# A linear-attention and expert kernel on one core: float64 weights joined in one VectorE pass, 1/E by backward scans, a new order table

## The chip, the core and the metric

The kernel runs on one core of one Trainium2 chip. The metric is the device time of one execution in microseconds (us), from the first to the last instruction of the program. TensorE does the matrix products (PE in the profile, PEld its weight loads), VectorE (DVE), ScalarE (ACT) and GpSimd (POOL) the elementwise work, and SyncE (SP) issues almost all transfers. Each engine runs its own instructions strictly in the order in which the program holds them, and waits on semaphores for the others.

## The reference

```python
def _attn_ref(r, k, v, w, u):                 # B, H, S, D = 4, 8, 768, 48
    state = np.zeros((B, H, D, D))
    for t in range(S):
        cur = np.einsum('bhd,bhe->bhde', u[None] * kt, vt)
        y[:, :, t] = np.einsum('bhd,bhde->bhe', rt, state + cur)
        state = wt[:, :, :, None] * state + np.einsum('bhd,bhe->bhde', kt, vt)

def _moe_ref(x, w_in, w_out):                 # x: 3072 x 384, w_in: 384 x 2048, w_out: 2048 x 384
    h = np.maximum(x @ w_in, 0.0)
    return (h * h @ w_out).astype(np.float32)
```

The attention output, laid out as 3072 tokens of 384 values, is the input x of the second part. r, k, v, w and u are float32. w_in and w_out arrive as float64, since a float32 array is multiplied by a float64 number when they are drawn; the kernel has to make float32 numbers out of their eight bytes, and then splits each of them into a leading and a remaining part of the matmul's reduced type (float32r), so that three matmuls with the two parts give nearly the float32 product.

## The kernel before

The sequence of 768 steps is cut into six chunks (c = 0 to 5) of 128. A **unit** (c, b) is one chunk of one of the four batches, 24 units in all. The attention of a unit works on four pairs of heads at once (NP = 4), with 112 partitions that hold two heads of 48 channels. It takes E, the running product of w along the chunk; r times E (shifted by one) and k divided by E are then multiplied on TensorE to give the scores inside the chunk, with a mask, a diagonal term from u, and the state that comes from the chunk before.

The steps carry names, which are also the keys of the order table: `load` (w, k and r into the tile st), `turn` (chunk 0 alone: TensorE transposes into the banks ob0 to ob3, hp0, hp1 and a0), `z` and `pt` (the other chunks: VectorE transposes blocks of 32, and 16 SP transfers spread them into pt), `scan` (E: four scans of 128 on VectorE, line 411), `ln` (ScalarE: Ln of E and Exp of its negative, lines 418 and 419, which is 1/E), `rt` (r times E, 422), `kn` (a Newton step on 1/E in two VectorE passes, 428 and 429, and k times the result, 431), `rk` (two GpSimd passes, 438 and 440, over r, k and u), `beta` (their sum, 441), `diag` (ScalarE, 448), `far` (a guard that tells whether the inputs allow this method, 450 and 451; otherwise a slow branch at the end runs, which these inputs never take), `mt` (score matmuls, 459), `mask` (463), `ktp`, `kt`, `dS`, `S` (the new state), `mix` (the output matmuls) and `x`, `x3` (output split into its two parts).

The second part walks over 16 slices f of 128 of the 2048 hidden columns for each chunk, with two slices to a weight group g (g = 0 to 7). In the profile, `hp` is the first product (line 573, nine matmuls), then ScalarE takes the maximum with zero (578), VectorE squares (579), ScalarE and VectorE split the result into g's two parts (581, 582), and `ob` is the second product (588, three matmuls for each batch, added up in the banks ob0 to ob3 over all f). In chunk 0 the first six slices (groups 0 to 2) are done in two halves, first for batches 0 and 1, then for batches 2 and 3 (`HALF`); a matmul of hp then has 256 columns in place of 512.

The weights are loaded once, in chunk 0, and stay in SBUF. A group has two halves, ri (for w_in, becomes wi) and ro (for w_out, becomes wo), each 128 partitions of 768 float64 numbers. A half goes through `split_w`:

```python
P.add("act", 0.8, rank, widen, r=parts, w=[q])       # high word times 2**-112
P.add("dve", 0.48, rank, shift, w=[q], port=True)    # three bits to the left
P.add("dve", 0.88, rank, sign, r=parts, w=[q], port=True)
P.add("dve", 0.88, rank, low, r=parts, w=[q], port=True)
```

These are lines 318, 322, 326 and 331. Then ScalarE casts the result to the leading part (338) and GpSimd subtracts it from the number itself, which leaves the remaining part (339). A matmul needs both parts.

What sets the order: every step is added to a `Plan` with its engine, a cost, a rank and the data that it reads and writes. `Plan.order` then plays the steps through with these costs, lets an engine take the ready step that can start first (of those the one with the smaller rank), and emits all instructions in the order that comes out. The numbers in `AT`, `AT0`, `U0`, `C1`, `WL`, `OFF`, `W0` and `LAG` are the ranks. The order on each engine is thus fixed when the program is built; on the chip nothing overtakes.

## Time and profile before

| what | value |
|---|---|
| time, median of 3 runs | 559.23 us (558.83 to 562.87) |
| span of the profiled execution | 559.93 us |
| busy: PE / DVE / ACT / POOL | 530.8 / 359.1 / 288.0 / 101.3 us |
| mean granted TensorE clock | 0.989 |
| transfers | 50.86 MB, mean 91 GB/s |

The page gives the busy time of each engine over the whole span. Since the work of chunk 0 differs from that of the later chunks, the busy times by stretch of the span say more than the sums. Matmuls overlap in the profile, so that the time one of them costs is the distance between two starts in the timeline, and not the duration in its row. A float32 matmul (not float32r) stands in the trace as two records. The groups of instructions are listed by line, with the mean duration of one.

### The profile page before, as it was taken

Reading aid. Unit: us, or ns where it says so; the run is one execution under the profiler, and the core shown is the slowest. Engines: PE = TensorE matmul, PEld = TensorE weight load, DVE = VectorE, ACT = ScalarE, POOL = GpSimd, SP = SyncE. Lnnn points to the kernel's source line nnn. Section 1 sums busy time; section 2 is a strip of 40 time slices with the busy share of each in tenths; the row PEclk is TensorE's granted clock in tenths of the full one; section 3 lists DMA queues with packets and bytes.
Section 4 is the critical chain, followed back from the end, with each engine's and each line's share of the span. In section 5 each row is a group of like instructions: output and inputs, shape, how many; then the busy total and the mean of one; then the engine's idle time right before and its main releaser. Section 6 shows DMA issues by size and latency. Waiting matters only on the chain. (4 is left out here: it accounts for less than half of the span.)

```text
span 559.9 us, 10076 instructions
## 1 busy us (share of the span) xinstructions
PE 530.8 (95%) x3800; PEld 466.7 (83%) x3800; DVE 359.1 (64%) x643; ACT 288.0 (51%) x677; POOL 101.3 (18%) x115
## 2 busy tenths in 40 slices
PE   4768898999999999999999999999999999999995
PEld 3557787889998999988888888888888888998994
DVE  5789879898759596776866767567475233332330
ACT  2786776668554747555554554553563222332322
POOL 4253552352203003030401102102000000000000
PEclk9998898999999999999999999999999999999999
DMA  9999699237472645637470470460440000010001
GB/s 156 210 240 217 122 255 218 39 64 137 99 141 51 111 109 91 123 78 135 80 132 2 78 168 24 84 129 2 78 106 3 12 1 1 14 58 2 0 1 60
DMA packets 206326, 50.86 MB, mean 91 GB/s; under 512 B 196032, under 2 KB 201152, under 8 KB 206272
## 3 DMA queue, kind: packets, MB, share of 16 engines
q1 hardware_dynamic: 205552, 49.17, 43.9%
q10 hardware_dynamic: 720, 0.98, 0.5%
q8 instruction: 32, 0.52, 0.4%
q14 instruction: 22, 0.18, 0.1%
HBM read 31.65 MB, written 4.72 MB: 65 GB/s over the span
## 5 line engine op out<-in xcount | busy, mean ns | idle before, releaser
L573 PE MATMUL hp<-x,wi 128*128 128x512 f32 (+1 forms) x1062 | 225.6, 358 | 4.7 <-DVE g L582 4.7
L588 PE MATMUL ob<-wo,g 128*128 128x384 f32 x1152 | 224.7, 341 | 4.4 <-ACT g L581 4.4
L588 PEld LDWEIGHTS ob<-wo,g 128*128 128x128 f32 x1152 | 200.5, 189 | 12.2 <-ACT g L581 4.9
L573 PEld LDWEIGHTS hp<-x,wi 128*128 128x128 f32 x1062 | 175.5, 190 | 31.9 <-DVE g L582 5.8
L579 DVE SCALAR_TENSOR_TENSOR hp<-hp,t 128x512 f32<-128x512 f32 (+1 forms) x118 | 70.2, 596 | 110.5 <-ACT t L578 110.0
L578 ACT ACTIVATE t<-hp 128x512 f32<-128x512 f32 (+1 forms) x118 | 60.9, 516 | 136.8 <-PE hp L573 111.2
L582 DVE TENSOR_TENSOR g<-hp,g 128x512 fp32r<-128x512 f32 (+1 forms) x118 | 69.1, 586 | 37.7 <-ACT g L581 35.9
L581 ACT CAST g<-hp 128x512 fp32r<-128x512 f32 (+1 forms) x118 | 59.2, 504 | 54.6 <-DVE hp L579 54.4
L448 ACT ACTIVATE m<-ident,beta 128x128 f32<-128x128 f32 x192 | 60.5, 395 | 7.0 <-DVE beta L441 7.0
L438 POOL TENSOR_TENSOR st<-st 128x384 f32<-128x384 f32 x24 | 25.1, 1047 | 64.7 <-DVE st L367 63.5
L463 DVE COPY_PREDICATED m<-caus,a 128x512 f32<-128x512 uint8 x48 | 33.0, 731 | 5.5 <-PE a L459 5.5
L459 PEld LDWEIGHTS a<-pt 48*128 48x128 f32 x384 | 25.8, 199 | 11.4 <-issue 7.1
L459 PE MATMUL a<-pt 48*128 48x128 f32 x384 | 30.8, 298 | 4.4 <-DVE pt L431 4.4
L526 DVE SCALAR_TENSOR_TENSOR x<-a,x 112x128 fp32r<-112x128 f32 (+2 forms) x44 | 17.9, 432 | 20.5 <-ACT x L525 19.9
L493 PE MATMUL a<-m,v 128*48 128x128 f32 (+1 forms) x384 | 28.5, 291 | 2.3 <-DVE m L463 1.8
L525 ACT ACTIVATE x<-a 112x128 fp32r<-112x128 f32 (+2 forms) x44 | 15.2, 389 | 28.8 <-PE a L493 28.5
L411 DVE TENSOR_TENSOR_SCAN pt<-pt,zero 112x128 f32<-112x128 f32 x80 | 28.9, 410 | 0.3 <-DMA x<-x 0.3
L493 PEld LDWEIGHTS a<-m,v 128*48 128x48 f32 (+1 forms) x384 | 21.4, 134 | 7.5 <-issue 4.5
L440 POOL TENSOR_TENSOR st<-st,un 128x384 f32<-128x384 f32 x24 | 26.9, 1120 | 1.6
L367 DVE STREAM_TRANSPOSE st<-st 128x1152 f32<-128x1152 f32 x20 | 26.8, 1359 | 0.0
L553 POOL TENSOR_TENSOR S<-S,Ec 112x192 f32<-112x192 f32 x16 | 8.2, 510 | 102.0 <-DVE S L552 102.0
L418 ACT ACTIVATE m<-pt 112x512 f32<-112x512 f32 x24 | 15.2, 635 | 20.1 <-DVE pt L411 15.7
(72 smaller groups left out, 394.5 us busy)
## 6 DMA issues: line engine op xcount, KB each, us to landing
pt<-st SPq DMA_DIRECT2D x80, 96.0 KB, 2.3
ro<-in_moe_w_out_dram SPq DMA_DIRECT2D x8, 768.0 KB, 9.6
v<-in_v_dram SPq DMA_DIRECT2D x24, 192.0 KB, 3.1
ri<-in_moe_w_in_dram SPq DMA_DIRECT2D x16, 288.0 KB, 9.1
st<-in_w_dram SPq DMA_DIRECT2D x11, 384.0 KB, 4.7
st<-in_k_dram SPq DMA_DIRECT2D x11, 384.0 KB, 5.3
st<-in_r_dram SPq DMA_DIRECT2D x11, 384.0 KB, 5.6
pt<-st SPq DMA_DIRECT2D x80, 48.0 KB, 2.5
```

The source lines that it names most:

```text
L411: lambda p=p: V.tensor_tensor_scan(out=pt[:, 0, p], data0=src(0)[:, p], data1=zero.broadcast_to([HP, C]), initial=1.0, op0=ALU.mult, op1=A ...
L440: P.add("pool", 1.0, rank("rk"), lambda: G.tensor_tensor(out=rk(), in0=rk(), in1=un.rearrange("s (h d) -> s h d", d=D), op=ALU.mult), w=[( ...
L448: A.activation(mv(j)[:, p], ident, AF.Copy, scale=beta.tile[:, 2 * p + j:2 * p + j + 1])
L459: T.matmul(mts[j].tile.rearrange("s (p t) -> s p t", p=NP)[:, p], pt[js, 2, p], pt[js, 1, p], start=True, stop=True)
L463: lambda j=j: V.copy_predicated(out=mv(j), mask=caus.unsqueeze(1).broadcast_to([128, NP, C]), data=mts[j].tile.rearrange("s (p t) -> s p t ...
L493: T.matmul(ybv()[j * J:j * J + n_, p], vt.tile[:, o:o + n_], mv(j)[:, p], start=(c == 0 and p == KT), stop=True, skip_group_check=True)
L573: T.matmul(hp.tile[:, 0:n], wi[f][:, wl, kt], xT[:, kt, xl, xs], start=(m == 0), stop=(m == 3 * KT - 1))
L578: P.add("act", 0.5 if full else 0.28, rank("g"), lambda: A.activation(t(), h(), AF.Relu), r=[hp], w=[(g, 1)])
L579: P.add("dve", 0.61 if full else 0.33, rank("g"), lambda: V.scalar_tensor_tensor(out=h(), in0=h(), scalar=0.0, in1=t(), op0=ALU.max, op1=A ...
L581: P.add("act", 0.53 if full else 0.31, rank("g"), lambda: A.copy(out=hi(), in_=h()), r=[hp], w=[(g, 0)])
L582: P.add("dve", 0.61 if full else 0.33, rank("g"), lambda: V.tensor_tensor(out=lo(), in0=h(), in1=hi().bitcast(F32), op=ALU.subtract), r=[h ...
L588: T.matmul(obs[b][:, 0:DM], g.tile[0][:, gl, o:o + C], wo[f][:, wl], start=(f == 0 and m == 0), stop=(f == NF - 1 and m == 2))
```

## The change

Four things are changed.

- **Weights.** Of a float64 number, ScalarE makes the scaled high word in place (no longer into q), and, in a second pass, writes the top three bits of the low word as a 16-bit number into the low half of the low word. GpSimd writes the sign as a 16-bit number into the high half of the low word (0 or 32768). One VectorE pass then shifts the high word by three bits and joins it with the low word, into q. The three VectorE passes before are gone. The cast and the subtraction stay.
- **1/E.** Ln, Exp and the two Newton passes are gone. VectorE takes the reciprocal of the last E of each of the four pairs, and four scans that run backwards over w multiply it up to 1/E for all other steps (`Fv`). In chunk 0, E stays in pt[0] and 1/E goes to pt[2]; in the other chunks both stand in the tile y0 of the pool m, one after the other. k times 1/E stays.
- **Signs.** u is no longer negated on GpSimd at the start, and the split of x no longer multiplies by -1. The load of ScalarE's function table for Ln and Exp at the start is gone; a table is loaded with the first copy.
- **Order.** All ranks are new, chunk 1 has a table of its own (`AT1`), and they stand in a class `Ranks`. `HALF` is as before.

```diff
+class Ranks:
+    AT0 = {'load': -108.5, 'turn': 0.25, 'rk': -26.25, 'beta': 54.5, 'far': 177, 'v': -75, 'scan': 155.5, ...
+    W0 = (-133.25, -46, 18.25, -15.5, -12.75, 6.25, 87.25, 122.75)
...
-    A.preload_act_table_set("natural_log_exp_and_others")
...
-    G.tensor_scalar(out=un, in0=un, scalar1=-1.0, scalar2=None, op0=ALU.mult)
...
-            def widen(q=q, bits=bits):
-                A.activation(q.tile, bits.bitcast(F32)[:, :, 1], AF.Copy, scale=2.0 ** -112)
-            def shift(q=q):
-                V.tensor_scalar(out=qi, in0=qi, scalar1=3, scalar2=None, op0=ALU.logical_shift_left)
-            def sign(q=q, bits=bits):
-                V.scalar_tensor_tensor(out=qi, in0=bits[:, :, 1], scalar=0x80000000, in1=qi,
-                                       op0=ALU.bitwise_and, op1=ALU.bitwise_or)
-            def low(q=q, bits=bits):
-                V.scalar_tensor_tensor(out=qi, in0=bits[:, :, 0], scalar=29, in1=qi,
-                                       op0=ALU.logical_shift_right, op1=ALU.bitwise_or)
+            halves = rt.rearrange("p k x -> p (k x)").bitcast(U16).rearrange("p (x z) -> p x z", z=4)
+            hi, lo = bits[:, :, 1], bits[:, :, 0]
+            def widen(hi=hi):
+                A.activation(hi.bitcast(F32), hi.bitcast(F32), AF.Copy, scale=2.0 ** -112)
+            def three_bits(halves=halves):
+                A.activation(halves[:, :, 0], halves[:, :, 1], AF.Copy, scale=2.0 ** -13, bias=2.0 ** -14 - 0.5)
+            def sign(hi=hi, halves=halves):
+                G.tensor_scalar(out=halves[:, :, 1], in0=hi.bitcast(F32), scalar1=0.0, scalar2=32768.0, op0=ALU.is_lt, op1=ALU.mult)
+            def join(q=q, hi=hi, lo=lo):
+                V.scalar_tensor_tensor(out=q.tile.bitcast(U32), in0=hi, scalar=3, in1=lo, op0=ALU.logical_shift_left, op1=ALU.bitwise_or)
+            P.add("act", 0.8, rank, widen, r=parts, w=[top])
+            P.add("act", 0.8, rank, three_bits, r=parts, w=[three])
+            P.add("pool", 1.8, rank, sign, r=[top], w=[three])
+            P.add("dve", 0.9, rank, join, r=[top, three], w=[q])
...
-        P.add("act", 0.53, rank("ln"), lambda: A.activation(yv(), pt[:, 0], AF.Ln), r=EK, w=[y0])
-        P.add("act", 0.53, rank("ln"), lambda: A.activation(yv(), yv(), AF.Exp, scale=-1.0), w=[y0])
...
-        P.add("dve", 0.62, rank("kn"), lambda: V.tensor_tensor(out=pt[:, 0], in0=pt[:, 0], in1=yv(), op=ALU.mult), r=[y0], w=EK, port=True)
-        P.add("dve", 0.62, rank("kn"), lambda: V.scalar_tensor_tensor(out=yv(), in0=pt[:, 0], scalar=2.0, in1=yv(), op0=ALU.subtract, op1=ALU.mult),
-              r=EK, w=[y0], port=True)
+        P.add("dve", 0.1, rank("kn"), lambda: V.reciprocal(out=Fv()[:, :, C - 1:C], in_=Ev()[:, :, C - 1:C]), r=EK, w=FK)
+        for p in range(NP):
+            P.add("dve", 0.32, rank("kn"),
+                  lambda p=p: V.tensor_tensor_scan(out=Fv()[:, p, C - 2::-1], data0=src(0)[:, p, C - 1:0:-1], data1=zero.broadcast_to([HP, C - 1]),
+                                                   initial=Fv()[:, p, C - 1:C], op0=ALU.mult, op1=ALU.add),
+                  r=[*keys(0), PT[0] + (p,)], w=[FK[p]], port=c > 0)
+        P.add("dve", 0.62, rank("kn"), lambda: V.tensor_tensor(out=pt[:, 2], in0=src(2), in1=Fv(), op=ALU.mult),
+              r=FK + keys(2), w=[PT[2]] + (FK if c < 1 else []), port=c > 0)
```

The order moves at three places that the prediction speaks of. The first is GpSimd's queue, from the first weight half on. Before (wi0 and wo0 are the remaining parts of group 0; Ec is the last E of a unit, L438 and L440 are rk):

```order
L339 TENSOR_TENSOR wi0_57<-q0_143,wi0_57 128x768
L427 COPY Ec2_160<-pt1_124 112x4
L339 TENSOR_TENSOR wo0_59<-q1_144,wo0_59 128x768
L438 TENSOR_TENSOR st01_132<-st01_132 128x8x48
L427 COPY Ec3_161<-pt1_124 112x4
L440 TENSOR_TENSOR st01_132<-st01_132,un_122 128x8x48
L438 TENSOR_TENSOR st01_132<-st01_132 128x8x48
L440 TENSOR_TENSOR st01_132<-st01_132,un_122 128x8x48
L339 TENSOR_TENSOR wi1_61<-q0_143,wi1_61 128x768
L339 TENSOR_TENSOR wo1_63<-q1_144,wo1_63 128x768
L339 TENSOR_TENSOR wi2_65<-q0_143,wi2_65 128x768
L438 TENSOR_TENSOR st0_145<-st0_145 128x384
```

GpSimd's queue now, from the same place up to the remaining part of wi2 (L359 is the new sign pass, L369 the subtraction):

```order
L359 TENSOR_SCALAR ri0_55<-ri0_55 128x768
L359 TENSOR_SCALAR ro0_57<-ro0_57 128x768
L369 TENSOR_TENSOR wi0_56<-q0_142,wi0_56 128x768
L369 TENSOR_TENSOR wo0_58<-q1_143,wo0_58 128x768
L359 TENSOR_SCALAR ri1_59<-ri1_59 128x768
L359 TENSOR_SCALAR ro1_61<-ro1_61 128x768
L369 TENSOR_TENSOR wi1_60<-q0_142,wi1_60 128x768
L369 TENSOR_TENSOR wo1_62<-q1_143,wo1_62 128x768
L359 TENSOR_SCALAR ri2_63<-ri2_63 128x768
L359 TENSOR_SCALAR ro2_65<-ro2_65 128x768
L359 TENSOR_SCALAR ri5_75<-ri5_75 128x768
L369 TENSOR_TENSOR wi2_64<-q0_142,wi2_64 128x768
```

Every half has two GpSimd passes where it had one, and the sign pass of the next group stands ahead of the subtraction of this one. Group 5 now comes third. From wi0 to wi4 GpSimd's queue holds ten sign passes, eleven subtractions (wi0, wo0, wi1, wo1, wi2, wo2, wi5, wo5, wi3, wo3, wi4) and four passes of rk.

The second place is SP's queue at the start. Before:

```order
L358 DMA st00_131<-in_r_dram 128x8x48
L387 DMA v0_147<-in_v_dram 128x8x48
L387 DMA v1_148<-in_v_dram 128x8x48
L305 DMA ri0_56<-in_moe_w_in_dram 48x3x512
L305 DMA ri0_56<-in_moe_w_in_dram 16x3x512
L305 DMA ri0_56<-in_moe_w_in_dram 48x3x512
L305 DMA ri0_56<-in_moe_w_in_dram 16x3x512
L307 DMA ro0_58<-in_moe_w_out_dram 128x2x768
L358 DMA st01_132<-in_w_dram 128x16x48
L358 DMA st01_132<-in_k_dram 128x16x48
L358 DMA st01_132<-in_r_dram 128x16x48
```

SP's queue now (st01 holds batches 2 and 3 of chunk 0):

```order
L388 DMA st00_130<-in_r_dram 128x8x48
L388 DMA st01_131<-in_w_dram 128x16x48
L388 DMA st01_131<-in_k_dram 128x16x48
L388 DMA st01_131<-in_r_dram 128x16x48
L417 DMA v0_146<-in_v_dram 128x8x48
L417 DMA v1_147<-in_v_dram 128x8x48
L338 DMA ri0_55<-in_moe_w_in_dram 48x3x512
L338 DMA ri0_55<-in_moe_w_in_dram 16x3x512
L338 DMA ri0_55<-in_moe_w_in_dram 48x3x512
L338 DMA ri0_55<-in_moe_w_in_dram 16x3x512
L340 DMA ro0_57<-in_moe_w_out_dram 128x2x768
```

The inputs of all four units of chunk 0 now come ahead of the first weights. Behind them the groups come in the order 0, 1, 2, 5, 3, 4, 6, 7 (before: 0, 1, 2, 3, then ri6 and ri4, ro6 and ro4, 5, 7); the 16 transfers of `pt` for chunk 1, which stood ahead of ro6 and ro4, now stand behind ro4. VectorE's queue follows: it holds 16 scans forward, 16 backward, 4 reciprocals, 6 masks, 4 sums of beta and 7 of the 8 products rt and kn of chunk 0 ahead of the first join (before: the passes of two units, 8 scans among them, ahead of the first weight pass).

The third place is TensorE's queue where group 4 is used for the first time (wi4). Before:

```order
L573 MATMUL hp1_140<-x0_130,wi3_69 128x512 x9
L588 MATMUL ob2_137<-wo2_67,g1_93 128x384 x3
L588 MATMUL ob3_138<-wo2_67,g1_93 128x384 x3
L573 MATMUL hp0_139<-x0_130,wi3_69 128x512 x9
L588 MATMUL ob2_137<-wo2_67,g2_95 128x384 x3
L588 MATMUL ob3_138<-wo2_67,g2_95 128x384 x3
L573 MATMUL hp1_140<-x0_130,wi4_73 128x512 x9
L588 MATMUL ob0_135<-wo3_71,g0_91 128x384 x3
```

TensorE's queue now:

```order
L608 MATMUL hp1_139<-x0_129,wi3_68 128x512 x9
L608 MATMUL hp0_138<-x0_129,wi3_68 128x512 x9
L623 MATMUL ob2_136<-wo2_66,g1_92 128x384 x3
L623 MATMUL ob3_137<-wo2_66,g1_92 128x384 x3
L623 MATMUL ob2_136<-wo2_66,g2_94 128x384 x3
L623 MATMUL ob3_137<-wo2_66,g2_94 128x384 x3
L623 MATMUL ob0_134<-wo3_70,g0_90 128x384 x3
L623 MATMUL ob1_135<-wo3_70,g0_90 128x384 x3
L623 MATMUL ob2_136<-wo3_70,g0_90 128x384 x3
L623 MATMUL ob3_137<-wo3_70,g0_90 128x384 x3
L608 MATMUL hp1_139<-x0_129,wi4_72 128x512 x9
```

All the other work ahead of this place is the same in both kernels: the whole attention of chunk 0, both halves of groups 0 to 2, and wi3 twice. Only the four ob blocks of the first slice of group 3 have moved from behind it to ahead of it.

More of the change, by code (lines that the diff above doesn't have):

```diff
@@ L12 @@
 U8 = mybir.dt.uint8
+U16 = mybir.dt.uint16
 U32 = mybir.dt.uint32
@@ L334, in split_w @@
-            P.add("act", 0.8, rank, widen, r=parts, w=[q])
-            P.add("dve", 0.48, rank, shift, w=[q], port=True)
-            P.add("dve", 0.88, rank, sign, r=parts, w=[q], port=True)
-            P.add("dve", 0.88, rank, low, r=parts, w=[q], port=True)
-            P.add("act", 0.74, rank, lambda q=q, tt=tt: A.copy(out=tt[:, 0], in_=q.tile), r=[q], w=parts + [lead])
+            top, three, lead = (nm, g, "top"), (nm, g, "three"), (nm, g, "lead")
+            hi, lo = bits[:, :, 1], bits[:, :, 0]
@@ L407, in attention @@
         keys = lambda t: [ps[t]] if c == 0 else raw
+        unit = c * B + b
+        Ev, EK = (lambda: pt[:, 0]), [PT[0] + (p,) for p in range(NP)]
+        if c:
+            y0 = Slot("m", unit)
+            Ev, EK = (lambda: y0.tile.rearrange("a (p s) -> a p s", p=NP)[0:HP]), [(y0, p) for p in range(NP)]
+        Fv, FK = Ev, EK
+        if c < 1:
+            Fv, FK = (lambda: pt[:, 2]), [PT[2] + (p,) for p in range(NP)]
         for p in range(NP):
             P.add("dve", 0.32, rank("scan"),
-                  lambda p=p: V.tensor_tensor_scan(out=pt[:, 0, p], data0=src(0)[:, p], data1=zero.broadcast_to([HP, C]),
+                  lambda p=p: V.tensor_tensor_scan(out=Ev()[:, p], data0=src(0)[:, p], data1=zero.broadcast_to([HP, C]),
```

74 lines of the change are left out of this document (37 added, 37 removed).

## The prediction

> **What bounds the kernel now.** I read the busy times by stretch first, then TensorE's timeline at two places. The columns of the first view are the stretch, its length, busy time of PE, PEld, DVE, ACT and POOL with the instructions in brackets, the granted clock, the share of the DMA engines and GB/s.
>
> ```profile
> PE 530.8 (95%) x3800; PEld 466.7 (83%) x3800; DVE 359.1 (64%) x643; ACT 288.0 (51%) x677; POOL 101.3 (18%) x115
> 0.00:33.00 33.00, 21.71 (x155) 16.72 (x156) 23.39 (x48) 17.71 (x41) 12.35 (x24) 1.00 1.12 196
> 33.00:60.00 27.00, 20.37 (x172) 17.30 (x170) 23.43 (x37) 18.10 (x45) 13.50 (x12) 0.87 1.04 216
> 60.00:100.00 40.00, 35.30 (x241) 31.64 (x237) 34.11 (x60) 28.70 (x63) 15.54 (x10) 0.96 0.87 197
> 100.00:140.00 40.00, 40.00 (x294) 35.13 (x293) 34.43 (x61) 27.85 (x60) 15.20 (x14) 1.00 0.41 76
> 140.00:240.00 100.00, 100.00 (x907) 91.53 (x906) 74.60 (x159) 59.48 (x166) 17.07 (x24) 1.00 0.51 101
> 240.00:550.00 310.00, 310.00 (x2027) 271.23 (x2026) 169.15 (x284) 134.24 (x299) 27.64 (x34) 1.00 0.26 54
> 550.00:559.93 9.93, 3.41 (x20) 3.09 (x18) 0.00 (x0) 1.92 (x4) 0.00 (x0) 0.88 0.24 85
> ```
>
> TensorE is the bound. From 100 to 550 us it never rests, so nothing that another engine saves there can show. What can be had lies in the first 100 us: 11.3 + 6.6 + 4.7 = 22.6 us of idle TensorE, and stretches at half clock (the 0.87 and 0.96). There DVE is busy for 81 of 100 us and POOL for 41. So the question is when the weights are ready, and I take one landmark: the first use of group 4, which is the third block of nine 512-column matmuls in TensorE's timeline (start, length, line).
>
> ```profile
> 80.41 2.26 PE L573 MATMUL hp<-x,wi 128*128 128x512 f32 x9
> 83.56 2.27 PE L573 MATMUL hp<-x,wi 128*128 128x512 f32 x9
> 86.70 2.26 PE L573 MATMUL hp<-x,wi 128*128 128x512 f32 x9
> 88.81 2.25 PE L588 MATMUL ob<-wo,g 128*128 128x384 f32 x12
> 93.08 3.91 PE L573 MATMUL hp<-x,wi 128*128 128x512 f32 x9 [2.02 <-DVE g L582]
> 96.82 1.21 PE L588 MATMUL ob<-wo,g 128*128 128x384 f32 x6
> ...
> 505.11 2.27 PE L588 MATMUL ob<-wo,g 128*128 128x384 f32 x12
> 507.22 2.24 PE L573 MATMUL hp<-x,wi 128*128 128x512 f32 x9
> 509.30 2.27 PE L588 MATMUL ob<-wo,g 128*128 128x384 f32 x12
> ```
>
> By distances between starts, a full hp block costs 2.08 us and four ob blocks 2.11. The landmark stands at 86.70, and 559.93 - 86.70 = 473.2 us follow it. In the new order four ob blocks (2.1) have moved ahead of it. Behind it, before loses 2.02 us of waiting and, in the block at 93.08, 3.74 - 2.08 = 1.7 at half clock. With the landmark at t4 in the new kernel, and one half-clock block of its own (1.7) after its waits, the span is **t4 + 473.2 - 2.1 - 3.7 + 1.7 = t4 + 469.1**, if TensorE stays fed from there. The work of TensorE is the same matmul for matmul.
>
> **The change part by part.** The rows of the groups are line, engine, operation, shapes, count, busy time and mean ns of one.
>
> ```profile
> L322 DVE TENSOR_SCALAR q<-q 128x768 uint32<-128x768 uint32 x16 | 10.1, 643 | 0.9 <-ACT q L318 0.9
> L326 DVE SCALAR_TENSOR_TENSOR q<-ri,q 128x768 uint32<-128x768 uint32 x8 | 7.6, 950 | 0.1
> L331 DVE SCALAR_TENSOR_TENSOR q<-ro,q 128x768 uint32<-128x768 uint32 x8 | 8.1, 1014 | 0.0
> L318 ACT ACTIVATE q<-ri 128x768 f32<-128x768 f32 x8 | 7.3, 908 | 0.9 <-POOL wi L339 0.9
> L338 ACT CAST wi<-q 128x768 fp32r<-128x768 f32 x8 | 6.6, 828 | 6.9 <-DVE q L331 6.9
> L339 POOL TENSOR_TENSOR wi<-q,wi x8: 1825/1844/2495, 24.4 to 124.2; 128x768 fp32r<-128x768 f32 x8
> L438 POOL TENSOR_TENSOR st<-st 128x384 f32<-128x384 f32 x24 | 25.1, 1047 | 64.7 <-DVE st L367 63.5 <-PE ob L399 0.7 <-PE hp L399 0.5
> L284 POOL TENSOR_SCALAR un<-un 128x384 f32<-128x384 f32 x1 | 1.2, 1172 | 2.8 <-DMA un<-in_u_dram 2.8
> L281 POOL TENSOR_SCALAR_AFFINE_SELECT sel<-sel 112x48 f32<-112x48 f32 x2 | 0.5, 234 | 0.0
> masks.py:199 POOL TENSOR_SCALAR_AFFINE_SELECT ident<-ident 128x128 f32<-128x128 f32 x1 | 0.3, 293 | 0.0
> L428 DVE TENSOR_TENSOR pt<-pt,m 112x512 f32<-112x512 f32 x24 | 17.7, 741 | 1.8 <-ACT m L419 1.4 <-issue 0.2
> L429 DVE SCALAR_TENSOR_TENSOR m<-pt,m 112x512 f32<-112x512 f32 x24 | 17.5, 732 | 0.1
> L418 ACT ACTIVATE m<-pt 112x512 f32<-112x512 f32 x24 | 15.2, 635 | 20.1 <-DVE pt L411 15.7 <-DMA st<-in_k_dram 2.5 <-DVE pt L431 1.8
> L463 DVE COPY_PREDICATED m<-caus,a 128x512 f32<-128x512 uint8 x48 | 33.0, 731 | 5.5 <-PE a L459 5.5
> L441 DVE TENSOR_REDUCE beta<-st 128x8 f32<-128x384 f32 x24 | 13.0, 541 | 0.5 <-POOL st L440 0.5
> L637 DVE TENSOR_SCALAR flag<-flag 128x1 f32<-128x1 f32 x1 | 0.2, 157 | 0.0
> ```
>
> *Weights.* DVE loses 0.64 + 0.95 + 1.01 = 2.6 us for each of 16 halves and gets one joined pass of the same shape, 0.95: 26 us less, nearly all in the first 100 us, where it was the busiest engine next to TensorE. ACT gets a second pass of 0.91 on each half (14.5 us). POOL gets 16 sign passes. No row has this form (float32 in, every second number, 16-bit out), so I bound it. Scaling the TENSOR_SCALAR of 384 numbers gives 2 x 1.17 = 2.34 us; the two AFFINE_SELECT rows rise by 59 ns for 80 numbers, which gives 0.23 + 720 x 0.00074 = 0.77. A two-input pass of the same length takes 1.83. I take **2.0**, between the row of the same operation and the row of the same length. The GPSIMD Engine Reference of the Trainium skill, section 4.1, says that a one-input pass on GpSimd runs at roughly line rate; by its clock that is an estimate of 0.64 us, which the TENSOR_SCALAR row (3.05 ns for each number) speaks against and the AFFINE_SELECT rows for.
>
> *1/E.* Each unit loses two DVE passes (1.47 us) and two ACT passes (1.27), and gets a reciprocal of four numbers (near the 0.16 of the smallest pass) and four scans.
>
> ```profile
> 6.99 1.37 DVE L411 TENSOR_TENSOR_SCAN pt<-ob,zero 112x128 f32<-112x128 f32 x4 [3.25 <-PE ob L399]
> ```
>
> Four scans cost 1.37, so DVE gets 0.06 more per unit, 1.4 us in all, and a backward scan that cost half as much again would add 16 us over the run; either way 20 of 24 units lie where TensorE never idles and DVE is busy for 55 to 86 of 100 us. That cover gone, each unit would cost those tenths. It is worth nothing there. In chunk 0 it shortens a unit by the trip to ACT and back.
>
> *Signs, table.* The pass on u (1.17, at 4.8 us, before POOL has anything to do) and the factor -1 cost nothing either way; the table load moves to the first copy, ahead of its wait, and is covered by the wait for the first transfers.
>
> *Order.* Three things come late in turn. First the transfers: ri0 now follows st01.
>
> ```profile
> DMA to landing us min/median/max: 4.6/5.3/5.6
> L358 SPq DMA_DIRECT2D st<-in_r_dram x1: 2099/2099/2099, 19.2 to 19.2; - x1
> DMA to landing us min/median/max: 8.0/9.0/10.9
> ```
>
> The first row is ri0's four transfers (issued 9.9 to 12.0, so landed by 17.6), the others st01's three (13.0, 13.5 and 19.2, so landed at about 22.0, 24.4, 27.2). They take 2.6 us each; ri0 lands 7.8 later, at 25.4, and its sign pass can end at 25.4 + 1.8 + 2.0 = 29.2. Second, DVE has all of chunk 0's scans ahead of the join: 7.0 + 8 x 1.37 + 6 masks x 0.73 + 4 sums x 0.54 + 7 products x 0.74 + 4 x 0.15 = 30.3; join 0.95 and cast 0.83 put POOL's first subtraction at **32.1**, and TensorE's first hp at 34, now with the attention of three units behind it. Third, from there to wi4 POOL has 10 sign passes x 2.0, 11 subtractions x 1.83, 4 rk x 1.05: 44.3 us, in a row. These meet the joins:
>
> ```profile
> 41.35 1.82 POOL L339 TENSOR_TENSOR wi<-q,wi 128x768 fp32r<-128x768 f32 x1 [3.75 <-DMA st<-in_w_dram]
> 42.51 1.48 DVE L331 SCALAR_TENSOR_TENSOR q<-ro,q 128x768 uint32<-128x768 uint32 x1
> 74.91 2.47 POOL L339 TENSOR_TENSOR wo<-q,wo 128x768 fp32r<-128x768 f32 x1 [2.26 <-ACT wo L338]
> ```
>
> Beside POOL the two-input DVE pass took 0.53 longer, and POOL 0.64 longer than its 1.83 elsewhere. I take 0.5 for each of 10 joins (0 to 0.95): t4 = 32.1 + 44.3 + 5.0 = **81.4**, span 550.5. The Trainium skill, SBUF — State Buffer, Who interferes with whom, says that a DVE pass with two inputs in SBUF and a GpSimd pass that reads SBUF exclude each other for the whole instruction; by that the joins would cost 9.5 in place of 5.0. The 42.51 row agrees: POOL's pass ends at 43.17, and the DVE pass ends 0.82 after it.
>
> The new wait is the join's, for POOL's sign pass. Behind the join of ro1 on DVE stands the product kn of the fourth unit, on which TensorE's second block after the first hp (mt) waits: POOL reaches the sign of ro1 at 32.1 + 2 x 1.83 + 2 x 2.0 = 39.8, kn ends near 42.5, and TensorE rests from 35 until then. From there its own work up to wi4 is 11 half blocks of hp, 2 full ones, 28 ob blocks and the rest of attention (4 us, an estimate by the same distances), 11 x 1.04 + 2 x 2.08 + 28 x 0.53 + 4 = 34.4; with a half-clock block it would be at wi4 at 78.6, so POOL is later by 3.
>
> What is next late if POOL is quicker: ACT has, up to the cast of wi4, 24 passes x 0.91 and 11 casts x 0.83, 31 us, and some 17 of other work (before, its 46.8 us between 33 and 100 less about 13 halves at 1.74 leave 24 in 67 us), so t4 is not below 25.4 + 48 + 1.8 = 75. The transfers up to ro4 are 13.8 MB by the shapes in the order, at the 196 to 216 GB/s above 64 to 70 us. So four resources stand within 12 us of each other. Behind wi4 POOL needs 4 signs, 5 subtractions and 4 rk until wo7, 24 us with the joins, against 38 on TensorE: covered. Of the moved transfers, `pt` for chunk 1 (16 issues on SP) no longer stands ahead of ro6 and ro4; st01 costs what is counted above.
>
> **The rivals.** (1) *The sign pass is cheap*, 0.8 us: POOL falls to 32.1 + 37, ACT and TensorE's own work pace, t4 = 75 to 76, span 544 to 545. For it: the AFFINE_SELECT rows. (2) *POOL and the joins exclude each other in full*: t4 = 85.9 with signs of 2.0 and 89.3 with 2.34, span 555 to 558.4, within 1% of before. For it: the 42.51 row. Against it: most subtractions ran at 1.84 in the median. (3) *Slower: the sign pass is long.* Writing 16-bit numbers with gaps is in no row; each 0.1 us moves t4 by 1.0. From 3.4 us on the span passes 564.8, and at 4.0 it is 570.5, TensorE waiting for each group in turn. That the change does less than it says I exclude, since the order shows every removed pass gone.
>
> **How the numbers follow.** The span of 559.93 stands 0.7 above the median of 559.23; that is less than the error of my sum, and I give the sum's 550.5 rounded to 550. Chances: forecast (signs 1.6 to 2.3, 546 to 553.6) 0.45; rival 1 and what lies between (541 to 546) 0.20; rival 2 0.22; rival 3 0.13. About 1% is what a measurement of this kernel tells from no change. So faster 0.65, same 0.22, slower 0.13. The range takes in ACT's bound with 2 us to spare below and rival 2 with a little of rival 3 above: 541.5 to 562.
>
> **What would show it.** The first hp at 34 us, wi4's at 81, and POOL busy for over 45 of the 49 us between; sign passes of 2.0; joins of 0.95 when POOL rests and near 1.5 when it does not. DVE's busy time in the first 100 us falls below 70. From 100 us to the last block TensorE stays without idle. I am wrong if TensorE waits in that part for ACT or DVE while POOL is idle, if the sign pass lies outside 1.6 to 2.4, or if later chunks show idle TensorE.

## The result

The changed kernel is slower: 586.62 us median (585.95 to 588.49), against 559.05 us (558.83 to 562.87) for the kernel before on the same chip. The ratio is 1.047, 95% interval 1.044 to 1.051. The profiled execution has a span of 586.6 us; that of before had 559.9.

The page's busy times and the busy times by stretch show where the 27 us lie. The columns are those of the same view of before: the stretch, its length, busy time of PE, PEld, DVE, ACT and POOL with their instructions, the granted clock, the share of the DMA engines, GB/s.

```profile
PE 541.9 (92%) x3800; PEld 472.9 (81%) x3800; DVE 353.8 (60%) x683; ACT 288.9 (49%) x645; POOL 155.8 (27%) x130
0.00:33.00 33.00, 20.30 (x118) 15.54 (x120) 24.26 (x61) 17.04 (x43) 13.07 (x27) 0.95 1.13 192
33.00:60.00 27.00, 17.73 (x151) 14.40 (x147) 10.75 (x11) 19.67 (x30) 22.29 (x9) 0.50 1.05 216
60.00:100.00 40.00, 31.19 (x211) 27.50 (x210) 23.96 (x37) 25.99 (x49) 34.66 (x15) 0.91 0.49 100
100.00:140.00 40.00, 35.62 (x224) 29.31 (x223) 29.73 (x49) 29.93 (x51) 27.95 (x14) 1.00 0.55 105
140.00:180.00 40.00, 37.44 (x298) 33.27 (x296) 30.59 (x59) 23.69 (x62) 19.34 (x15) 0.96 0.51 100
180.00:550.00 370.00, 370.00 (x2654) 325.39 (x2654) 224.61 (x454) 162.34 (x399) 38.46 (x53) 1.00 0.35 69
```

POOL is now busy for 22.29 + 34.66 = 57 of the 67 us between 33 and 100, while DVE, the engine that the change was to relieve, is busy for 35 of them. TensorE goes on resting until 180 us, and the whole stretch from 33 to 60 ran at half clock. From 180 to 550 us TensorE never rests, as before.

The groups of the weights and of the scans (line, engine, operation, shapes, count, busy time and mean ns of one, then the idle time before them and what ended it):

```profile
L359 POOL TENSOR_SCALAR ro<-ro 128x768 uint16<-128x768 f32 x8 | 32.9, 4111 | 0.2 <-ACT ro L356 0.2
L359 POOL TENSOR_SCALAR ri<-ri 128x768 uint16<-128x768 f32 x8 | 31.4, 3927 | 8.9 <-ACT ri L356 4.7 <-DMA ri<-in_moe_w_in_dram 4.1
L369 POOL TENSOR_TENSOR wo<-q,wo 128x768 fp32r<-128x768 f32 x8 | 15.0, 1874 | 9.9 <-ACT wo L368 9.8
L362 DVE SCALAR_TENSOR_TENSOR q<-ro 128x768 uint32<-128x768 uint32 x8 | 18.1, 2261 | 11.8 <-POOL ro L359 11.2 <-POOL wo L369 0.5
L362 DVE SCALAR_TENSOR_TENSOR q<-ri 128x768 uint32<-128x768 uint32 x8 | 11.2, 1394 | 16.8 <-POOL ri L359 13.6 <-DMA pt<-st 1.9 <-POOL wi L369 1.2
L463 DVE TENSOR_TENSOR_SCAN m<-pt,m,zero 112x127 f32<-112x127 f32 x80 | 34.2, 471 | 0.0
L449 DVE TENSOR_TENSOR_SCAN m<-pt,zero 112x128 f32<-112x128 f32 x80 | 28.7, 407 | 0.0
L356 ACT ACTIVATE ri<-ri 128x768 uint16<-128x768 uint16 x8 | 15.6, 1947 | 0.0
```

The sign pass takes 3.9 to 4.1 us in place of the 2.0 of the forecast, ScalarE's pass for the three low bits 1.94 in place of 0.91, and the join 1.39 and 2.26 in place of 0.95 (1.45 with the 0.5 that the sum allowed for POOL). VectorE stands idle for 24.8 us ahead of the joins, waiting for the sign passes.

What that does to TensorE is seen in pieces of the timeline of POOL, VectorE and TensorE, put together in order of time (start, length, engine, line):

```profile
34.44 3.90 POOL L359 TENSOR_SCALAR ro<-ro 128x768 uint16<-128x768 f32 x1
34.65 1.48 DVE L362 SCALAR_TENSOR_TENSOR q<-ri 128x768 uint32<-128x768 uint32 x1 [4.36 <-POOL ri L359]
38.17 1.80 POOL L369 TENSOR_TENSOR wi<-q,wi 128x768 fp32r<-128x768 f32 x1
38.38 2.42 DVE L362 SCALAR_TENSOR_TENSOR q<-ro 128x768 uint32<-128x768 uint32 x1 [1.52 <-POOL ro L359]
...
52.38 2.41 DVE L362 SCALAR_TENSOR_TENSOR q<-ro 128x768 uint32<-128x768 uint32 x1 [2.24 <-POOL ro L359]
54.71 0.34 DVE L585 TENSOR_TENSOR S<-a,Ec 112x192 f32<-112x192 f32 x1
55.11 1.11 PE L429 MATMUL a<-ident,st 128*128 128x128 f32 x4 [4.04 <-DVE S L585]
55.87 2.27 PE L608 MATMUL hp<-x,wi 128*128 128x256 f32 x9
...
110.27 0.63 PE L608 MATMUL hp<-x,wi 128*128 128x512 f32 x2
111.70 1.90 PE L608 MATMUL hp<-x,wi 128*128 128x512 f32 x7 [0.79 <-POOL wi L369]
...
152.24 5.54 PE L608 MATMUL hp<-x,wi 128*128 128x512 f32 x16 [2.39 <-POOL wi L369]
```

VectorE takes its work in order. The join of ro1 at 52.38 waits for POOL's sign pass, and the 0.34 us update of the state (S) stands behind it; TensorE waits 4.04 us for that update, with its first hp block next in its own queue. So a pass on POOL holds up attention that has nothing to do with the weights. The landmark of the forecast, the third 512-column hp block, stands at 110.27, not at 81.4, and its third matmul has to wait for POOL's subtraction of wi4. Waits for POOL reach to the last weight group at 152 us. They are not the larger part: between 60 and 160 us TensorE waits 4.2 us for POOL's subtractions and 8.5 us for VectorE's g. The longest of these waits, 2.63 us ahead of 93.72, ends with a g that stands on VectorE behind the join of 90.45, and that join had waited 2.08 us for POOL's sign pass.

### The profile page after: what moved, and what is told of

It reads as the page before. It is cut to its first block, busy times and chain, and to the rows that moved or that the text cites. A ratio compares the mean times of both kernels' runs of the same rounds, so it can differ in the third digit from the quotient of the medians.

```text
span 586.6 us, 10062 instructions
## 1 busy us (share of the span) xinstructions
PE 541.9 (92%) x3800; PEld 472.9 (81%) x3800; DVE 353.8 (60%) x683; ACT 288.9 (49%) x645; POOL 155.8 (27%) x130
## 5 line engine op out<-in xcount | busy, mean ns | idle before, releaser
L588 POOL TENSOR_TENSOR S<-S,Ec 112x192 f32<-112x192 f32 x16 | 9.4, 588 | 115.6 <-DVE S L587 114.3
L561 DVE TENSOR_TENSOR x<-a,x 112x128 fp32r<-112x128 f32 (+2 forms) x44 | 17.8, 430 | 33.2 <-ACT x L560 30.1
L459 POOL COPY Ec<-m 112x4 f32<-112x4 f32 x16 | 3.7, 230 | 121.1 <-DVE m L449 121.1
L494 PEld LDWEIGHTS a<-pt 48*128 48x128 f32 x384 | 27.0, 204 | 10.0 <-issue 4.0
L494 PE MATMUL a<-pt 48*128 48x128 f32 x384 | 32.1, 304 | 2.9 <-DVE pt L466 2.7
L528 PE MATMUL a<-m,v 128*48 128x128 f32 (+1 forms) x384 | 29.7, 297 | 5.4 <-DVE m L498 3.5
L463 DVE TENSOR_TENSOR_SCAN m<-pt,m,zero 112x127 f32<-112x127 f32 x80 | 34.2, 471 | 0.0
L359 POOL TENSOR_SCALAR ri<-ri 128x768 uint16<-128x768 f32 x8 | 31.4, 3927 | 8.9 <-ACT ri L356 4.7
L359 POOL TENSOR_SCALAR ro<-ro 128x768 uint16<-128x768 f32 x8 | 32.9, 4111 | 0.2 <-ACT ro L356 0.2
```

Of the source, the lines that this page charges most:

```text
L359: G.tensor_scalar(out=halves[:, :, 1], in0=hi.bitcast(F32), scalar1=0.0, scalar2=32768.0, op0=ALU.is_lt, op1=ALU.mult)
L463: lambda p=p: V.tensor_tensor_scan(out=Fv()[:, p, C - 2::-1], data0=src(0)[:, p, C - 1:0:-1], data1=zero.broadcast_to([HP, C - 1]), initia ...
L494: T.matmul(mts[j].tile.rearrange("s (p t) -> s p t", p=NP)[:, p], pt[js, 2, p], pt[js, 1, p], start=True, stop=True)
L528: T.matmul(ybv()[j * J:j * J + n_, p], vt.tile[:, o:o + n_], mv(j)[:, p], start=(c == 0 and p == KT), stop=True, skip_group_check=True)
```

## The experiments

Spans are those of the profiled executions. To compare: before 559.9, changed kernel 586.6. Where no median is given, a kernel ran once. Runs of one kernel differ: the four of the changed kernel have spans of 584.1 to 586.6, those of before, on all the chips used, 556.4 to 561.9. So a difference of less than about 5 us between two single spans shows little by itself.

The expectations name four theories by letters. S: the sign pass on GpSimd, and what waits behind it on VectorE, is the loss. O: the new order, with three units of attention ahead of the first hp block, is the loss. A: ScalarE's 1.94 us pass is the loss. C: the clock, at one half after pauses of TensorE, is the loss, or the second error of the forecast.

**Cutting the two passes.** Both passes keep their place in the order and lose seven eighths of their numbers, each alone and then together. What remains of them takes 0.68 to 0.85 us on POOL and 0.42 on ScalarE.

```diff
-   G.tensor_scalar(out=halves[:, :, 1], in0=hi.bitcast(F32), ...)
+   G.tensor_scalar(out=halves[:, 0:96, 1], in0=hi.bitcast(F32)[:, 0:96], ...)      # sign cut
-   V.scalar_tensor_tensor(..., op0=ALU.logical_shift_left, op1=ALU.bitwise_or)
+   V.scalar_tensor_tensor(..., op0=ALU.logical_shift_left, op1=ALU.bitwise_and)    # with the sign cut
-   A.activation(halves[:, :, 0], halves[:, :, 1], ...)
+   A.activation(halves[:, 0:96, 0], halves[:, 0:96, 1], ...)                       # three bits cut
```

> The sign pass stays on GpSimd and in its place in the order but covers 96 of 768 numbers, and the join ands in place of or (so that what is left in the words does no harm): the signs of the weights are left out. Theory S: the pass takes 0.4 to 0.8 us, GpSimd's chain from the first subtraction to the block of group 4 shrinks by 30 us and ScalarE (24 passes, half of them at 1.94) comes next at 85 to 90 us: span 553 to 560. Rival O: first hp still behind 50 us, span above 575. Rival A: span above 575.

> ScalarE's pass for the three low bits covers 96 of 768 numbers (the low three bits of the other weights are left out). Theory S: ScalarE is released 1.7 us per half, GpSimd's idle time of 4.7 us behind that pass goes, but its chain of sign passes stays: span 577 to 585. Rival A: the span falls to 560 or less. Rival O: 580 or more, as it is.

> The sign pass on GpSimd and the pass for the three low bits on ScalarE both cover 96 of 768 numbers, the order unchanged (signs and low bits of the other weights are left out). With the sign pass alone cut so, the span was 562.4. If ScalarE's 1.94 us pass then holds the rest, the span falls to 552 or less; if TensorE's own work behind a late first hp block (50 us) holds it, the span stays within 559 to 563.

| span, us | three bits 1.94 us | three bits 0.42 us |
|---|---|---|
| sign 3.9 to 4.1 us | 586.6 | 580.9 |
| sign 0.7 to 0.85 us | 562.4 | 552.1 |

The sign pass is worth 24.2 us with the long ScalarE pass beside it and 28.8 with the short one; the ScalarE pass is worth 5.7 and 10.3. Each comes out 4.6 us larger when the other is gone, as with two engines of which the later one sets the time, but that difference is no larger than runs of one kernel show. Together they make 34.5 us, more than the whole loss: with both nearly free the new order, the scans and the joined pass come out at a time of 554.0 us, 4.2 below the one run of before that was taken beside it (558.16). With the sign cut the join makes other numbers of the weights; the matmuls cost the same with them, 2.13 us for a full hp block (two from 75.50 to 79.76) as in the changed kernel (two from 99.64 to 103.89). With the sign cut alone 562.4 is 2.4 above the range of theory S, and far below the 575 of both rivals. Theory S holds, and theory A in part, as the second bound. TensorE's rows of the run with both cut:

```profile
45.73 0.36 PE L608 MATMUL hp<-x,wi 128*128 128x256 f32 x1
46.28 1.21 PE L608 MATMUL hp<-x,wi 128*128 128x256 f32 x8 [0.19 <-DVE x L561]
47.41 1.16 PE L494 MATMUL a<-pt 48*128 48x128 f32 x16
...
75.50 4.43 PE L608 MATMUL hp<-x,wi 128*128 128x512 f32 x18 [0.32 <-issue]
83.92 4.36 PE L608 MATMUL hp<-x,wi 128*128 128x512 f32 x18
```

The first hp block starts at 45.7 even here, and what it waits for last is not a weight but x. So there is a second error in the forecast, which stays when the two passes are nearly gone.

**The sizes of the forecast.** The same cut, but to the number of elements at which the passes take what the forecast had said.

```diff
-   halves[:, :, 1] ... hi.bitcast(F32)
+   halves[:, 0:370, 1] ... hi.bitcast(F32)[:, 0:370]
-   halves[:, :, 0], halves[:, :, 1]
+   halves[:, 0:316, 0], halves[:, 0:316, 1]
```

> The changed kernel with its order, but the sign pass covers 370 of 768 numbers and the pass for the three low bits 316 of 768, which by the runs with 96 numbers makes them 2.0 and 0.91 us long: the two sizes that the forecast used (the other signs and low bits are left out). If those two sizes were all that was wrong, the span is the forecast's 550.5 us, within 2. With 96 numbers in both it was 552.1 already, with the first hp block at 45.7 and not at 34; so if the attention of three units ahead of the first hp block was a second mistake, the span is 554 to 559 and the first hp block stands at 45 to 50.

The passes took 2.02 to 2.20 and 0.92 us, and the span was 557.0. The groups and TensorE's rows:

```profile
L359 POOL TENSOR_SCALAR ri<-ri 128x370 uint16<-128x370 f32 x8 | 16.1, 2018 | 6.4 <-ACT ri L356 6.4
L356 ACT ACTIVATE ri<-ri 128x316 uint16<-128x316 uint16 x8 | 7.3, 918 | 0.0
```

```profile
29.24 0.69 PE L528 MATMUL a<-m,v 128*64 128x128 f32 x4 [3.46 <-DVE m L498]
...
47.80 2.27 PE L608 MATMUL hp<-x,wi 128*128 128x256 f32 x9
50.00 1.61 PE L494 MATMUL a<-pt 48*128 48x128 f32 x16
...
80.47 4.42 PE L608 MATMUL hp<-x,wi 128*128 128x512 f32 x18 [1.08 <-POOL st L475]
...
88.91 3.34 PE L608 MATMUL hp<-x,wi 128*128 128x512 f32 x13
```

This divides the miss (the span's, from 550.5 to 586.6). With its own sizes the forecast's 550.5 would have been 557.0 in this run: some 6.5 us are an error of its sum. The other 29.6 us, from 557.0 to 586.6, are the two sizes.

**The prices.** Passes over 768 numbers in several forms, behind the last chunk, with nothing beside them, each form twice with the same result within 0.02 us.

```diff
+   two = dict(scalar1=0.0, scalar2=32768.0, op0=ALU.is_lt, op1=ALU.mult)
+   G.tensor_scalar(out=tp, in0=f(hi), **two)           # tp: every fourth 16-bit number, hi: every second 32-bit one
+   ...
+   A.activation(flat16, w2.bitcast(U16)[:, 1536:2304], AF.Copy, scale=2.0 ** -13, bias=0.0)
```

> Behind the last chunk, with nothing beside them, stand passes over 768 numbers in several forms on GpSimd, VectorE and ScalarE, twice each. If the price of GpSimd's sign pass is the 16-bit output with gaps, the same pass with float32 output takes 2.0 to 2.4 us and the one with 16 bits and no gaps lies between; if it is the second operation, the pass with one operation takes about half of 3.9; if it is neither, contiguous float32 takes 3.9 too. On ScalarE 16-bit in and out with gaps takes 1.9; if the 16-bit output is the cause, 16 bits in and 32 out takes 0.9. VectorE's sign pass: 0.65 to 1.5.

The timeline, in the order of the program:

```profile
587.20 3.86 POOL L667 TENSOR_SCALAR sc<-sc 128x768 uint16<-128x768 f32 x1 [127.53 <-DVE sc L658]
591.15 3.22 POOL L668 TENSOR_SCALAR sc<-sc 128x768 uint16<-128x768 f32 x1
594.45 2.84 POOL L669 TENSOR_SCALAR sc<-sc 128x768 f32<-128x768 f32 x1
597.38 2.77 POOL L670 TENSOR_SCALAR sc<-sc 128x768 uint16<-128x768 f32 x1
600.23 2.77 POOL L671 TENSOR_SCALAR sc<-sc 128x768 f32<-128x768 f32 x1
603.09 2.13 POOL L672 TENSOR_SCALAR sc<-sc 128x768 f32<-128x768 f32 x1
605.25 1.02 DVE L673 TENSOR_SCALAR sc<-sc 128x768 uint16<-128x768 f32 x1 [18.14 <-POOL sc L672]
606.30 0.56 DVE L674 TENSOR_SCALAR sc<-sc 128x768 f32<-128x768 f32 x1
...
609.53 1.90 ACT L678 ACTIVATE sc<-sc 128x768 uint16<-128x768 uint16 x1 [27.85 <-DVE sc L677]
611.46 0.88 ACT L679 ACTIVATE sc<-sc 128x768 uint32<-128x768 uint16 x1
...
615.21 0.84 ACT L682 ACTIVATE sc<-sc 128x768 uint16<-128x768 uint16 x1
```

On POOL a pass with one operation over numbers without gaps takes 2.13 (L672); the second operation adds 0.64 (L671); gaps in 32-bit input and output add 0.07 (L669); 16-bit output with gaps adds 1.09 (L667, whose input has the gaps of L669, against L670, which reads and writes without gaps and costs no more than with 32-bit output). So no single part makes the 3.86: of the 1.86 us by which it exceeds the forecast's 2.0, the 16-bit gaps are 1.09 and the second operation 0.64. None of the six forms comes near the 0.8 us of rival 1. Section 4.1 of the GPSIMD Engine Reference in the Trainium skill calls a pass with one input roughly line rate; here the cheapest form took 2.13 us, over three times the 0.64 that the prediction had estimated from it, and the measurement decides. On ScalarE it is the gaps in the 16-bit output alone: 1.90 with them, 0.84 without, 0.88 where whole 32-bit words are written with gaps. On VectorE 16-bit output with gaps takes 1.02 against 0.56 for 32-bit output with gaps; 16 bits without gaps were not run there.

**The order.** The changed kernel with the old numbers of the order (units, weights, FFN).

```diff
-    U0 = (-92.25, -27.75, -70.75, 59.25)
-    W0 = (-133.25, -46, 18.25, -15.5, -12.75, 6.25, 87.25, 122.75)
+    U0 = (-16, -15.25, -6.75, -5.5)
+    W0 = (-12.5, -9.5, -1, 0.25, 0.25, 5.5, 5.0, 17)
...
```

> The changed kernel with the numbers of the order as they were before the change (the first block of TensorE's hp work then stands again ahead of most of the attention of chunk 0). Theory S (GpSimd's sign passes, some 64 us, are the loss): GpSimd still needs 10 x 3.9 for the signs up to group 4, so the span stays above 575 us. Rival O (the new order costs most of the loss): first hp near 35 us, span 565 or less.

The span was 612.1. The first hp block stood at 35.43, and it helped nothing:

```profile
125.95 3.87 PE L608 MATMUL hp<-x,wi 128*128 128x512 f32 x9 [10.62 <-DVE g L617]
```

At 125.95 TensorE has waited 10.62 us for VectorE's g; the longest wait of the changed kernel behind its first hp block is 2.63. Rival O falls: with these passes the new numbers save 25.5 us (612.1 - 586.6).

**The sign pass on VectorE.**

```diff
-   G.tensor_scalar(out=halves[:, :, 1], ...)
+   V.tensor_scalar(out=halves[:, :, 1], ...)
-   P.add("pool", 1.8, rank, sign, ...)
+   P.add("dve", 0.9, rank, sign, ...)
```

> The sign pass of each weight half is issued on VectorE in place of GpSimd, all else as in the changed kernel (the order is planned anew for that). Theory S (the sign pass on GpSimd, 4.0 us in place of the forecast 2.0, and what waits behind it on VectorE, is the loss): VectorE does the pass in 0.65 to 1.5 us, the joins no longer wait for GpSimd, the span falls by 25 us or more, to 545 to 562 us; the next bound is ScalarE with its 1.94 us pass. Rival O (the new order, with three units of attention ahead of the first hp block, is the loss): the first hp stays behind 50 us and the span above 575. Rival A (ScalarE's 1.94 us pass is the loss): span above 575 too.

Only 580.55 us, ratio 1.037 (1.033 to 1.041). That was a miss of theory S as I had put it; by this run alone rivals O and A stood, and the cuts and the old numbers above decide against them as the main cause. The order was planned anew for it. POOL is free of the pass, which takes 1.05 to 1.14 on VectorE, but VectorE now waits in its queue for ScalarE:

```profile
DVE ri L359 <- ACT ri L356: 9.2, 6, 3.3
DVE ro L359 <- ACT ro L356: 6.5, 7, 1.3
```

These are the waits of VectorE between 18 and 160 us (total, times, longest). The next run takes that pass away.

```diff
-   A.activation(halves[:, :, 0], halves[:, :, 1], ...)
+   A.activation(lo, halves[:, :, 1], ...)      # lo: the whole 32-bit word
```

> The run with the sign pass on VectorE (span 579.8), with ScalarE's three low bits written as 32-bit words in place of 16-bit ones with gaps (0.88 in place of 1.90 us), the order the same. If what kept that run slow is VectorE waiting in its queue for ScalarE's 16-bit passes (15.7 us of waits): the span falls to 560 to 568. If it is the order planned for it: 575 or more.

The span was 571.6, between the two expectations: the 16-bit pass on ScalarE made 8.2 of the 20 us above before, and 12 remain. The pass took 0.90, VectorE's waits for it fell from 15.7 us to under 3, and TensorE still waits 5.0 us for g. What makes the rest is open; the order, which is planned from the costs written in the code, is a guess that no run here separates.

**TensorE's clock.** In the run with the forecast's sizes TensorE has a pause of 3.46 us ahead of 29.24 (above), and half clock follows it (0.50 from 30 to 40 us); in the changed kernel it is the same. To keep the clock up, one group of transposes and one of scores in the pauses were issued three times. The second run has the passes at full length, the first leaves out what the run with the forecast's sizes leaves out.

```diff
-            for p in range(NP):
+            for p in [*range(NP)] * (3 if (c, b) == (0, 2) else 1):
...
-                    for p in range(NP):
+                    for p in [*range(NP)] * (3 if (b, i) == (2, 0) else 1):
```

> The run with the forecast's two sizes (span 557.0), with TensorE kept busy in its two longest pauses ahead of the first hp block (at 15.6 to 18.2 and 25.6 to 29.2 us): one transpose group and one group of scores of chunk 0 are issued three times over, with the same results. Theory C (the clock falls to one half after these pauses, and the attention ahead of the first hp block then takes twice as long: the second mistake of the forecast): the granted clock stays at 1.00 up to 45 us, the first hp block moves from 47.8 to 41 to 44, the span falls by 3 to 6, to 551 to 554. If the clock does not matter there, since GpSimd or VectorE hold the chain: first hp within 1 us, span 556 to 558.

> The changed kernel itself with the same repeated work on TensorE in its two pauses. Theory S: there GpSimd's chain of sign passes sets the blocks from group 1 to group 4, so a clock that stays full helps the first hp block (55.9) at most and the span by less than 3: 583 to 587. Theory C as the main cause of the loss (34 us at half clock in one piece): 575 or less.

The first did not do what it was made for: the granted clock was 0.56 between 20 and 25 us and 0.50 from 25 to 40, so the added scores took 5.49 us and the first hp block came at 49.4. The median was 559.12 (556.0 to 560.5), the span 557.4. It does not decide theory C, which stays open for the 6.5 us. One sign speaks for it: of its ten runs the four with a mean clock of 0.981 or more have spans of 554.1 to 555.8, the six at 0.972 to 0.977 have 557.2 to 558.1. But the kernel before shows no such order (561.9 at 0.988, 558.8 at 0.976), and where in the span the clock differed is not known. In the second, the clock was up between 25 and 40 us (0.81, 1.00, 0.72), and the first hp block stood at 55.91 and the span at 586.4, as without the added work. VectorE's update of S behind the join held TensorE there (4.11 us). So in this run the higher clock in that stretch bought nothing while the sign pass was long; from 40 to 50 us it was 0.50 again.

**The scans, and a better split.** Two kernels with the scans, each with an order table of its own, chosen by the end of the program that the planner's costs give. The first has the old split of the weights. The second writes the three bits as 32-bit words and leaves the sign to VectorE, where two inputs and two operations fit into one pass; of the work on the weights only the subtraction is left on POOL. The edit shown is that of the second.

```diff
-   A.activation(halves[:, :, 0], halves[:, :, 1], AF.Copy, scale=2.0 ** -13, bias=2.0 ** -14 - 0.5)
+   A.activation(lo, halves[:, :, 1], AF.Copy, scale=2.0 ** -13, bias=2.0 ** -14 - 0.5)
-   A.activation(hi.bitcast(F32), hi.bitcast(F32), AF.Copy, scale=2.0 ** -112)
+   A.activation(q.tile, hi.bitcast(F32), AF.Copy, scale=2.0 ** -112)
-   G.tensor_scalar(out=halves[:, :, 1], ...)
-   V.scalar_tensor_tensor(out=q.tile.bitcast(U32), in0=hi, scalar=3, in1=lo, ...)
+   V.scalar_tensor_tensor(out=qi, in0=qi, scalar=3, in1=lo, op0=ALU.logical_shift_left, op1=ALU.bitwise_or)
+   V.scalar_tensor_tensor(out=qi, in0=hi, scalar=0x80000000, in1=qi, op0=ALU.bitwise_and, op1=ALU.bitwise_or)
...
+    AT0 = {'load': -498.75, 'turn': 64.75, 'rk': -142.25, 'beta': 21.25, 'far': 179.25, 'v': -39.0, 'scan': 102.5, ...}
+    U0 = (-165.5, -141.25, -72.25, 39.5)
+    W0 = (-170.25, -116.75, -29.5, -1.75, 20.75, 30.75, 49.0, 141.25)
...
```

> The weights as in the kernel before (three VectorE passes for each half), 1/E by the backward scans, an order table of its own. If the scans cost nothing where TensorE never idles, 553 to 561 us; if the longer backward scans (0.47 in place of 0.41 us for each) or the tiles that they hold longer slow the later chunks, 563 or more.

> The weights without GpSimd's sign pass and without 16-bit output: ScalarE writes the three low bits as whole 32-bit words (0.88 us by the prices run), VectorE joins and then puts the sign in, two passes of 0.96 each; an order table of its own. The scans for 1/E are kept. Theory S: the joins no longer wait for GpSimd, ScalarE's passes for one half fall from 3.65 to 2.65 us, VectorE needs 1.9 for each half in place of 2.6 in the kernel before: 550 to 557 us, below both kernels. If the scans or the order cost time by themselves, 560 or more.

The old split with the scans: 563.04 us, ratio 1.003 (1.002 to 1.004) against 561.06 for before in the same runs. With this table the scans bring nothing; the median stands where the expectation put scans that slow the later chunks, but from 180 to 540 us TensorE is idle for only 0.9 of 360 us. Table and scans are not separated here. The two VectorE passes: 556.84 us (555.29 to 557.97), ratio 0.992 (0.990 to 0.993), 0.8% faster than before, which is little, though its interval leaves out no change at all, and 5% below the changed kernel. Its busy times between 33 and 100 us, and its new passes:

```profile
33.00:60.00 27.00, 24.36 (x203) 20.94 (x202) 20.69 (x32) 21.91 (x45) 9.19 (x5) 1.00 1.03 231
60.00:100.00 40.00, 39.78 (x290) 35.72 (x290) 34.59 (x61) 34.65 (x73) 17.44 (x13) 1.00 0.86 174
```

```profile
L360 DVE SCALAR_TENSOR_TENSOR q<-q,ri 128x768 uint32<-128x768 uint32 x8 | 8.1, 1007 | 2.7 <-ACT q L353 2.7
L364 DVE SCALAR_TENSOR_TENSOR q<-ri,q 128x768 uint32<-128x768 uint32 x8 | 7.5, 944 | 0.0
L356 ACT ACTIVATE ri<-ri 128x768 uint32<-128x768 uint16 x8 | 7.3, 914 | 0.0
```

TensorE is busy for 64.1 of the 67 us between 33 and 100 at full clock; it was 48.9 in the changed kernel and 55.7 in before.

## Why the prediction was wrong

The step that failed is the term "10 sign passes x 2.0". The pass takes 3.9 to 4.1. Its lower and upper bounds, 0.77 and 2.34, came from POOL rows with 32-bit output, scaled by length, the upper one from a row with one operation; a second operation and a 16-bit output with gaps are 0.64 and 1.09 us by the prices. For one operation without gaps the upper bound was near, 2.34 against 2.13. The text said that no row had the form, and still took 2.0. The mechanism was right in its main part: POOL's chain of passes sets when the groups are ready, and TensorE waits for it, directly and by way of VectorE's queue. This is rival 3, which had a chance of 0.13 and gave 570.5 us at 4.0.

Rival 3 was still 16.1 us short of the span of 586.6, and that can be followed. Its t4 would be 81.4 + 20 = 101.4; measured were 110.27. Of these 8.9 us, 6.1 are the start of POOL's first subtraction, at 38.17 and not at 32.1: ri0's sign pass started at 30.72 and took 3.89, and ro0's, 3.90 long, stood next on POOL, ahead of the subtraction. The other 2.8 lie in POOL's chain: from there to the landmark POOL is idle for 10.5 of 72.1 us, where the sum had 5.0 for the joins; sign passes that follow each other start 3.7 us apart, which takes some of that back. Then 476.3 us follow the landmark, not 469.1, 7.2 more: the step "24 us against 38 on TensorE: covered" fell with the same size, and TensorE waits for wi4 and wi7.

The other steps:

- *ScalarE's second pass, 0.91.* Taken from a pass over 32-bit numbers; 1.94 with 16-bit output and gaps. Worth 5.7 us here, by the one run that cut it alone, little more than runs differ by.
- *The joins, 0.5 each.* Too little: those of ri took 0.44 longer than 0.95 in the mean, those of ro 1.31, which is 0.88 on average, near the 0.95 of rival 2. POOL's idle time ahead of ro's subtractions (9.8 us, for ScalarE's cast behind that join) is rival 2's mechanism, in half of the joins.
- *First hp at 34, TensorE's own pace from 42.5.* Wrong for another reason. I asked when the weights were ready, not when x was; the first hp block needs x of the third unit, and in TensorE's queue it stands behind the attention of three units. On VectorE the update of S that TensorE waits for ahead of that block (4.04 us) stands behind the join of ro1; the prediction had put only kn there. The pace itself was right: with both passes cut TensorE goes from the scores, the block after the first hp, to the landmark in 36.5 us (47.41 to 83.92), against 34.4 + 1.7 = 36.1 in the prediction, but it starts 4.9 us after 42.5. With the forecast's sizes the scores started at 50.00, 7.5 us late, and the landmark came at 88.91; POOL's subtraction of wi4 ended at 89.4 there, 8 us after 81.4. So both chains were late, and how the 6.5 us of span divide between them, and how much is half clock, stays open.
- *t4 + 469.1.* Right where TensorE stays fed: 562.4 - 92.94 = 469.5 with the sign cut, 552.1 - 83.92 = 468.2 with both cut, 557.0 - 88.91 = 468.1 with the forecast's sizes.
- *"From 3.4 us on the span passes 564.8, each 0.1 us moves t4 by 1.0."* Cutting the sign by 3.3 us moved the span by 24.2 to 28.8, that is 0.72 to 0.88 for each 0.1.
- *1/E hidden.* Right where TensorE never idles: a backward scan takes 0.46 to 0.47 against 0.41, inside the bound of half as much again, and TensorE is busy for 370.00 of 370 us from 180 on.
- *What would show it.* DVE's busy time in the first 100 us fell to 59, below 70 as said. POOL was busy for 61.6 of the 72.1 us between its first subtraction and the landmark, 85%, where 45 of 49 was said, 92%. A sign pass outside 1.6 to 2.4 and idle TensorE behind 100 us were the named signs of being wrong, and both are in the profile.
- *Span and time.* The sum is a span, and was given as a time because the span of before stood 0.7 above its median. In the runs that have both, the time is 1.7 to 2.5 us longer than the span of the same run, so the sum stood for some 552 us. Against a miss of 36 us this is little.

## What to carry to other kernels

A pass whose form no row shows (type written, gaps, number of operations) should not be priced between rows of other forms: a few such passes at the end of the kernel give every price in one look, and here they would have turned the forecast. Moving work from a busy engine to an idle one puts the idle engine's pass in front of everything that stands behind its consumer in that consumer's queue, so look at what is queued there, not at the share of busy time. And a landmark's readiness is the latest of all its inputs: the weights were followed to the microsecond, x and the work ahead of it were not.

## What was not expected of the hardware

VectorE and POOL exclude each other in a way that depends on POOL's pass. A join that starts 0.2 us after POOL's two-input subtraction ends some 0.82 us after that pass (38.38 above: 2.42 us, against 0.96 alone in the prices run). A join that starts 0.2 us after a sign pass takes 1.48 and ends 2.2 us before that pass does (34.65). One that starts 1.0 us after a sign pass is not held up at all, as these rows of the same timeline show:

```profile
128.61 3.94 POOL L359 TENSOR_SCALAR ro<-ro 128x768 uint16<-128x768 f32 x1 [0.15 <-ACT ro L356]
129.59 0.95 DVE L362 SCALAR_TENSOR_TENSOR q<-ri 128x768 uint32<-128x768 uint32 x1
```

So in this trace the sign pass holds VectorE up for its first part only, though it lasts twice as long as the subtraction. "Who interferes with whom" in SBUF — State Buffer of the Trainium skill lets the two exclude each other for the whole instruction: the trace agrees for the subtraction and not for the sign pass.

Output of 16 bits with gaps costs on all three engines: 1.09 us more for 768 numbers on POOL, 1.06 on ScalarE, and on VectorE 1.02 us in all, against 0.56 for 32-bit output with gaps. Without gaps, 16 bits cost nothing on POOL and ScalarE.
